# A linear-attention layer and a soft mixture of experts on one core: load ring, weight order and output queues changed

## The chip, the core and the metric

The kernel runs on one core of a Trainium2 chip. The metric is the device time of one execution in microseconds; a profile of one execution shows its span, that is the time from its first to its last instruction. The core has five engines that run side by side and wait for one another by semaphores: TensorE (PE, matrix products; PEld are its weight loads), VectorE (DVE), ScalarE (ACT), GpSimd (POOL) and SyncE (SP). SyncE, ScalarE and GpSimd can issue DMA transfers, which move data between HBM and the on-chip memory SBUF on 16 shared DMA engines. Matrix products land in PSUM.

## The reference

Two layers in a row. The first is a linear attention with decay, for 4 batches, 8 heads, 768 steps and head size 48 (float32):

```python
for t in range(S):
    kt, vt, rt = (k[:, :, t], v[:, :, t], r[:, :, t])
    cur = np.einsum('bhd,bhe->bhde', u[None] * kt, vt)
    y[:, :, t] = np.einsum('bhd,bhde->bhe', rt, state + cur)
    state = w[None, :, :, None] * state + np.einsum('bhd,bhe->bhde', kt, vt)
```

Its output, as 3072 rows x of 384, goes through a soft mixture of 8 experts with 4 slots each (phi is 384 x 32, w1 8 x 384 x 1024, w2 8 x 1024 x 384):

```python
logits = x @ phi
d = softmax of logits over the 3072 rows      # dispatch
slot_input = d.T @ x                          # 32 slots of 384
h = np.maximum(slot_input[e] @ w1[e], 0.0)    # for each expert e
slot_out[e] = h @ w2[e]
c = softmax of logits over the 32 slots       # combine
out = c @ slot_out
```

The two softmax lines are shortened here. All of x must be known before the experts can start, and the experts must be done before the first row of the output.

## The kernel before

**Stage 1, the chunks.** The 3072 rows are worked in 12 chunks of 256 rows (`nS`; three to a batch), two neighbouring rows to a partition (`J` = 2). The main loop (`for n in range(nS - 1)`, L538, and a tail for the last chunk) is software-pipelined: in iteration n it computes chunk n, prepares the transposes of n+1 and the products of n+3, and routes the rows of n-1. The order on each engine is that of the program. For each chunk:

- `mults` (L241) scales r, k by powers of the decay (L254, L256) and k by u (L257), on GpSimd, for chunk 0 on VectorE. `v_cast` (L264, ScalarE) makes v bf16. `r_copy`, `kur` and `dsum` (L277, L283, L294) form the term of the row with itself, and `dmul` (L301) its product with v. After `dsum` and `v_cast` nothing reads the loaded chunk any more.
- `trans` and `evac` transpose the scaled r and k (TensorE, ScalarE); `att` and `masks` (L331, L343) make the masked products within the chunk; `y_open`, `inter`, `state`, `intra` and `st_next` build the output and the state.
- `xt`, `lg`, `expo` make the logits of the rows and their exponentials; `disp` (L488, L491) adds the chunk's share to the slot inputs. There the rows x are the stationary operand of the matmul, loaded into TensorE 128 contiguous columns at a time.

**Loads.** r, k and v come by SyncE, in runs of 384 bytes. The pool `ld` has two buffers of a whole batch each. Batch 0 is loaded in nine transfers, one per chunk and tensor (`load_part`, L75), batches 1 to 3 in three each (`load`, L83). A later batch reuses the buffer of the batch two before it, so it waits for the last chunk of that one. The order is k, r, v.

**Weights.** w1 and w2 are read as float32 and cast to bf16 by transfers that GpSimd issues between its products (`load_w`), 0.79 MB of bf16 each: 8 blocks of w1, 7 of w2 and the last of w2 in four parts. How many go out at which iteration stands in the lists `W_IN` (inside `mults`) and `W_AT` (at the iteration's end); at iteration 8 all the rest. w2 of experts 4 to 7 (`w2_tail`) goes into a batch buffer of `ld`. For w1, input column `mo*128 + p` lies on partition p, so that each partition gets three runs of 4 KB; w2 has one run of 12 KB.

**Stage 2, the experts** (from `up`, L645): the up projections of four experts at a time (`up`, L652), transposes (`turn`), the down projections (`down`, L681), and the last expert's apart (`last_down`, L712), in the order in which its four parts land. `fill` and `keep` are padding matmuls on TensorE whose results nobody reads.

**Stage 3, the output:** 12 pieces of 256 rows. TensorE multiplies the combine weights by the slot outputs, VectorE scales the even rows of a piece (L745) and ScalarE the odd ones (L747), and SyncE sends it out, the first piece in two transfers (L749), the others in one of 384 KB (L751). The pool `ob` has six buffers.

Of the kernel before, what the change touches and what calls it, by code (L numbers as in the profile page):

```python
# [11 lines left out]
def kernel(  # L12
# [12 lines left out]
    nc = tc.nc  # L25
    B, H, S, D = r.shape
# [16 lines left out]
    P = 128  # L43
# [14 lines left out]
    w2_h = [wts.tile([P, E // 2, nF, Dm], bf, name="w2_h")[:]]  # L58
    ident = wts.tile([P, P], bf, name="ident")
    ld = ctx.enter_context(tc.tile_pool(name="ld", bufs=2))  # L60
    cst = ctx.enter_context(tc.tile_pool(name="cst", bufs=1))

    loads = {}

    SRC = ((1, k), (0, r), (2, v))

    def new_batch(b):
        bt = ld.tile([P, 3, H, nSb, J * D], f32, name="rkv")
        for i in range(nSb):
            loads[b * nSb + i] = [bt[:, x, :, i, :].rearrange("p h (j d) -> p j h d", j=J) for x in range(3)]  # L70
        return bt

    def load_part(bt, i):
        for x, src in SRC:
            nc.sync.dma_start(out=bt[:, x, :, i, :],  # L75
                              in_=src[0, :, i * TS:(i + 1) * TS, :].rearrange("h (p j) d -> p h (j d)", j=J))

    def load(b):
        if b >= B:
            return  # L80
        bt = new_batch(b)
        for x, src in SRC:
            nc.sync.dma_start(out=bt[:, x].rearrange("p h i m -> p (h i) m"),  # L83
                              in_=src[b].rearrange("h (i p j) d -> p (h i) (j d)", p=P, j=J))

    b_first = new_batch(0)
    load_part(b_first, 0)
# [14 lines left out]
    for i in range(1, nSb):  # L102
        load_part(b_first, i)
    load(1)
# [71 lines left out]
    w1_ap = moe_w1.rearrange("e (mo p) f -> p e mo f", p=P)  # L176
# [12 lines left out]
    def w2_load(e, f0=0, f1=nF):  # L189
        if e == XE and f0 == 0:  # L190
            tail = ld.tile([P, (E - XE) * nF * Dm], bf, name="w2_tail", tag="rkv",
                           padded_shape=[P, 3 * H * nSb * 2 * J * D])
            w2_h.append(tail[:].rearrange("p (e f d) -> p e f d", e=E - XE, f=nF))
        nc.gpsimd.dma_start(out=w2_h[e // XE][:, e % XE, f0:f1, :], in_=w2_ap[:, e, f0:f1, :])
# [5 lines left out]
    for f in range(0, nF, 2):  # L200
        w_todo.append((w2_load, (E - 1, f, f + 2)))
# [8 lines left out]
    with tc.tile_pool(name="wk", bufs=2) as wk, \  # L210
# [270 lines left out]
        def disp(n):  # L481
# [3 lines left out]
            for g in range(2):  # L485
                q = 2 * (n % 2) + g
                for mi in range(nM):
# [39 lines left out]
        dsum(0)  # L527
        mults(1)
        mults(2)
        load_w(2)  # L530
        trans(0, "kk")
        evac(0, "kk")
        trans(0, "rr")
# [248 lines left out]
```

## Time and profile before

| | us |
|---|---|
| median of 13 runs (lowest to highest) | 128.74 (127.67 to 137.31) |
| the profiled execution | 128.7 |
| its span | 126.5 |
| busy: PE / DVE / ACT / POOL | 98.0 / 92.3 / 78.9 / 77.7 |
| r, k, v, w1, w2 read (with the output, HBM read 39.38 MB, written 4.72 MB) | mean 349 GB/s over the span |

The profile gives for each engine its busy time and for each group of instructions its line, engine, operation and shapes. The slices cut the span into 40 equal parts; a digit is a share in tenths. Windows give the same for chosen stretches. An idle time stands in brackets after an instruction, with what ended it. The DMA rate counts what arrives, so a weight that is cast from float32 to bf16 counts with half of the bytes that were read. The DMA share can pass 1[...].

### The profile page before, as it was taken

Reading aid. Unit: us, or ns where it says so; the run is one execution under the profiler, and the core shown is the slowest. Engines: PE = TensorE matmul, PEld = TensorE weight load, DVE = VectorE, ACT = ScalarE, POOL = GpSimd, SP = SyncE. Lnnn points to the kernel's source line nnn. Section 1 sums busy time; section 2 is a strip of 40 time slices with the busy share of each in tenths; the row PEclk is TensorE's granted clock in tenths of the full one; section 3 lists DMA queues with packets and bytes.
Section 4 is the critical chain, followed back from the end, with each engine's and each line's share of the span. In section 5 each row is a group of like instructions: output and inputs, shape, how many; then the busy total and the mean of one; then the engine's idle time right before and its main releaser. Section 6 shows DMA issues by size and latency. Waiting matters only on the chain.

```text
span 126.5 us, 4177 instructions
## 1 busy us (share of the span) xinstructions
PE 98.0 (77%) x1779; PEld 70.5 (56%) x1779; DVE 92.3 (73%) x180; ACT 78.9 (62%) x143; POOL 77.7 (61%) x70
## 2 busy tenths in 40 slices
PE   3994899969597969079798959997999999794000
PEld 3493577756576757067676748775666566521000
DVE  5499988899999999385999997999662411375500
ACT  5869495869697967378688878788222320375500
POOL 6009999799998899997999999993410000000000
PEclk9999999999999999955999996799869999996555
DMA  3999999999999999999999999999999999049993
GB/s 83 301 325 324 334 327 271 310 212 230 286 301 282 235 256 265 343 296 267 243 253 254 239 211 225 216 213 219 214 211 212 218 204 167 4 150 394 400 401 154
DMA packets 23543, 31.78 MB, mean 251 GB/s; under 512 B 10450, under 2 KB 18132, under 8 KB 23524
## 3 DMA queue, kind: packets, MB, share of 16 engines
q0 software_dynamic: 4816, 12.63, 51.4%
q1 hardware_dynamic: 18288, 18.88, 47.0%
q8 instruction: 14, 0.23, 0.7%
q10 hardware_dynamic: 420, 0.00, 0.2%
q14 instruction: 5, 0.04, 0.1%
HBM read 39.38 MB, written 4.72 MB: 349 GB/s over the span
## 4 chain that ended last, share of the span: by engine, by line
PE 35%; DMA 23%; DVE 20%; SPq 8%; ACT 5%; issue 3%; ACTq 1%; DVEq 0%
DMA rkv<-in_v_dram 14%; SPq L83 8%; DMA out_dram<-o_s 6%; DVE at_s L343 6%; PE t_p L312 5%; DVE rpun L294 5%; PE aat_p L331 4%; DMA w_pd<-in_w_dram 3%; DVE dv L301 3%; PE xl_p L431 3%; DVE rkv L283 3%; PE y_p L352 2%; PE pad L517 2%; PE so_p L681 2%; PE rpun L488 2%
## 5 line engine op out<-in xcount | busy, mean ns | idle before, releaser
L343 DVE TENSOR_TENSOR at_s<-aat_p,mask 128x512 bf16<-128x512 f32 x47 | 30.2, 684 | 3.8 <-PE aat_p L331 3.6
L254 POOL TENSOR_TENSOR rr<-rkv,W_n 128x768 bf16<-128x768 f32 x11 | 20.0, 1822 | 9.1 <-DMA rkv<-in_r_dram 9.0
L257 POOL TENSOR_TENSOR rkv<-rkv,u_rep 128x768 f32<-128x768 f32 x11 | 19.9, 1809 | 0.9
L256 POOL TENSOR_TENSOR kk<-rkv,W_k 128x768 bf16<-128x768 f32 x11 | 20.0, 1818 | 0.1
L331 PE MATMUL aat_p<-t_rr,t_kk 64*64 64x128 bf16 x376 | 12.5, 249 | 9.0 <-ACT t_kk L319 6.3
L277 ACT COPY rpun<-rkv 128x384 f32<-128x384 f32 x23 | 11.3, 492 | 9.4 <-PE rpun L491 7.8
L331 PEld LDWEIGHTS <-t_kk 64*64 64x64 bf16 x384 | 8.7, 123 | 12.3 <-ACT t_kk L319 8.5
L301 DVE TENSOR_TENSOR dv<-v_bf,rpun 128x768 bf16<-128x768 bf16 x12 | 11.4, 954 | 3.1 <-ACT v_bf L264 2.1
L319 ACT COPY t_kk<-t_p 128x1024 bf16<-128x1024 bf16 x12 | 12.2, 1013 | 1.1 <-PE t_p L312 1.1
L283 DVE TENSOR_TENSOR rkv<-rkv,rpun 128x384 f32<-128x384 f32 x23 | 12.6, 546 | 0.2
L294 DVE TENSOR_REDUCE rpun<-rkv 128x16 f32<-128x768 f32 x12 | 11.5, 961 | 0.4
L264 ACT CAST v_bf<-rkv 128x768 bf16<-128x768 f32 x12 | 10.0, 830 | 2.9 <-DMA rkv<-in_v_dram 2.9
L319 ACT COPY t_rr<-t_p 128x1024 bf16<-128x1024 bf16 x11 | 11.2, 1017 | 0.5 <-PE t_p L312 0.3
L382 PE MATMUL s_p<-v_bf,kk 64*128 64x96 bf16 x160 | 11.4, 218 | 0.0
L391 DVE TENSOR_TENSOR st<-s_p,wm 128x384 bf16<-128x384 f32 x20 | 10.9, 546 | 0.5 <-PE s_p L382 0.3
L433 ACT COPY xt_s<-xl_p 128x768 bf16<-128x768 bf16 x11 | 8.8, 798 | 3.1 <-PE xl_p L431 3.0
L382 PEld LDWEIGHTS <-kk 64*128 64x128 bf16 x160 | 8.3, 102 | 3.8 <-issue 3.8
L745 DVE TENSOR_SCALAR o_s<-o_p,rsum_r 128x384 f32<-128x384 f32 x12 | 7.0, 615 | 4.3 <-DMA out_dram<-o_s 3.7
L412 ACT CAST x_t<-y_p 128x384 bf16<-128x384 f32 x22 | 9.6, 494 | 0.0
L747 ACT ACTIVATE o_s<-o_p,rsum_r 128x384 f32<-128x384 f32 x12 | 6.4, 584 | 4.7 <-DMA out_dram<-o_s 4.0
L488 PE MATMUL rpun<-Lexp,x_t 128*128 128x32 bf16 x66 | 5.2, 180 | 5.1 <-DVE dv L301 5.1
L312 PE MATMUL t_p<-ident,kk 128*128 128x128 bf16 x96 | 8.9, 248 | 0.2 <-ACT t_rr L319 0.2
(130 smaller groups left out, 188.0 us busy)
## 6 DMA issues: line engine op xcount, KB each, us to landing
w_all<-in_moe_w_dram POOLq DMA_DIRECT2D x8, 768.0 KB, 11.8
out_dram<-o_s SPq DMA_DIRECT2D x11, 384.0 KB, 4.3
w_h<-in_moe_w_dram POOLq DMA_DIRECT2D x4, 768.0 KB, 13.2
w_tail<-in_moe_w_dram POOLq DMA_DIRECT2D x3, 768.0 KB, 19.5
rkv<-in_k_dram SPq DMA_DIRECT2D x3, 384.0 KB, 4.4
rkv<-in_r_dram SPq DMA_DIRECT2D x3, 384.0 KB, 4.7
rkv<-in_v_dram SPq DMA_DIRECT2D x3, 384.0 KB, 5.0
w_tail<-in_moe_w_dram POOLq DMA_DIRECT2D x4, 192.0 KB, 21.0
```

The lines of the kernel that those rows point to most:

```text
L254: nc.gpsimd.tensor_mul(rr[:, :, :, 0:D], r_l, W_n[:])
L256: nc.gpsimd.tensor_mul(kk[:, :, :, 0:D], k_l, W_k[:])
L257: nc.gpsimd.tensor_mul(ku, ku, u_b)
L277: nc.scalar.copy(rp, loads[n][0][:, j, :, :])
L283: nc.vector.tensor_mul(s["ku"][:, j, :, :], s["ku"][:, j, :, :], s["rps"][j])
L294: nc.vector.tensor_reduce(d, s["ku"], axis=mybir.AxisListType.X, op=ALU.add)
L301: nc.vector.tensor_mul(dv[:], s["v"][:], d[:, :, :, None].to_broadcast([P, J, H, D]))
L312: nc.tensor.transpose(t_p[:, q, :, j, :], s[nm][:, j, 2 * q:2 * q + 2, :].rearrange("p h d -> p (h d)"), ident[:])
L319: nc.scalar.copy(t_s[:], s.pop("p_" + nm)[:])
L331: nc.tensor.matmul(at_p[a][g * HF:(g + 1) * HF, q, :], kT[sl, q, g, j, :], rT[sl, q, g, :, :].rearrange("p j c -> p (j c)"), start=True, s ...
L343: nc.vector.tensor_mul(s["at"][:, a, j, :, :], at_p[a][:], mask[:, j, None, :].to_broadcast([P, nP, P]))
L382: nc.tensor.matmul(s_p[:, q * D2:(q + 1) * D2], s["kk"][sl, j, 2 * q:2 * q + 2, :].rearrange("p h d -> p (h d)"), s["v"][sl, j, 2 * q:2 * ...
```

## The change

Five things change together.

- The pool `ld` becomes a ring of six buffers of one chunk each. A chunk is loaded by three transfers (for the first chunk k, r, v, for the others r, k, v). Six chunks are asked for at the start, chunk 6 after `v_cast(0)`, and chunk n+7 at the end of iteration n. w2 of experts 4 to 7 takes four buffers of the ring.
- Weights are issued at other iterations: one block instead of two before the loop, and new lists `W_IN` and `W_AT`. The last block of w2 comes in three parts (4, 2 and 2 of 8 columns of F/128), and `last_down` takes the first four in one go.
- Column `p*3 + mo` of the input now lies on partition p for w1, so each partition gets one run of 12 KB. To match it, the dispatch matmuls take every third column of x as stationary operand.
- Output pieces 2, 4, 6, 8 and 10 are sent by GpSimd, the others by SyncE, and `ob` has 12 buffers.
- Each half of the first output piece is scaled in two column halves, one on VectorE and one on ScalarE.

```diff
-    w2_h = [wts.tile([P, E // 2, nF, Dm], bf, name="w2_h")[:]]
+    w2_h = wts.tile([P, E // 2, nF, Dm], bf, name="w2_h")
+    w2_of = [w2_h[:, e] for e in range(E // 2)]
-    ld = ctx.enter_context(tc.tile_pool(name="ld", bufs=2))
+    ld = ctx.enter_context(tc.tile_pool(name="ld", bufs=6))
...
-    def load(b):
-        if b >= B:
-            return
-        bt = new_batch(b)
-        for x, src in SRC:
-            nc.sync.dma_start(out=bt[:, x].rearrange("p h i m -> p (h i) m"),
-                              in_=src[b].rearrange("h (i p j) d -> p (h i) (j d)", p=P, j=J))
-
-    b_first = new_batch(0)
-    load_part(b_first, 0)
+    def load(n):
+        if n >= nS:
+            return
+        b, i = divmod(n, nSb)
+        bt = ld.tile([P, 3, H, J * D], f32, name="rkv")
+        loads[n] = [bt[:, x].rearrange("p h (j d) -> p j h d", j=J) for x in range(3)]
+        for x, src in SRC if n == 0 else (SRC[1], SRC[0], SRC[2]):
+            nc.sync.dma_start(out=bt[:, x],
+                              in_=src[b, :, i * TS:(i + 1) * TS, :].rearrange("h (p j) d -> p h (j d)", j=J))
+
+    load(0)
...
-    for i in range(1, nSb):
-        load_part(b_first, i)
-    load(1)
+    for n in range(1, NL):
+        load(n)
...
-    w1_ap = moe_w1.rearrange("e (mo p) f -> p e mo f", p=P)
+    w1_ap = moe_w1.rearrange("e (p mo) f -> p e mo f", p=P)
...
     def w2_load(e, f0=0, f1=nF):
-        if e == XE and f0 == 0:
-            tail = ld.tile([P, (E - XE) * nF * Dm], bf, name="w2_tail", tag="rkv",
-                           padded_shape=[P, 3 * H * nSb * 2 * J * D])
-            w2_h.append(tail[:].rearrange("p (e f d) -> p e f d", e=E - XE, f=nF))
-        nc.gpsimd.dma_start(out=w2_h[e // XE][:, e % XE, f0:f1, :], in_=w2_ap[:, e, f0:f1, :])
+        if e >= XE and f0 == 0:
+            tail = ld.tile([P, nF * Dm], bf, name="w2_tail", tag="rkv", padded_shape=[P, 2 * 3 * H * J * D])
+            w2_of.append(tail[:].rearrange("p (f d) -> p f d", f=nF))
+        nc.gpsimd.dma_start(out=w2_of[e][:, f0:f1, :], in_=w2_ap[:, e, f0:f1, :])
...
-    for f in range(0, nF, 2):
-        w_todo.append((w2_load, (E - 1, f, f + 2)))
+    for f0, f1 in ((0, 4), (4, 6), (6, nF)):
+        w_todo.append((w2_load, (E - 1, f0, f1)))
...
+                x_v = x_of[n][g].rearrange("p (c m) -> p m c", m=nM)
                 for mi in range(nM):
-                    nc.tensor.matmul(un_p[:, mi * ES:(mi + 1) * ES], x_of[n][g][:, mi * P:(mi + 1) * P], le[:, q, :],
+                    nc.tensor.matmul(un_p[:, mi * ES:(mi + 1) * ES], x_v[:, mi, :], le[:, q, :],
...
-        W_IN = [0, 0, 1, 0, 0, 1, 1, 1, 1]
-        W_AT = [0, 0, 1, 0, 0, 1, 1, 1, 3, 0, 0]
+        W_IN = [0, 0, 1, 0, 1, 1, 1, 1, 1]
+        W_AT = [0, 0, 0, 0, 1, 1, 1, 1, 2, 0, 0]
...
-        load_w(2)
+        load_w(1)
...
         v_cast(0)
+        load(NL)
...
-            if n % nSb == 1:
-                load(n // nSb + 2)
+            load(n + 1 + NL)
...
-        last_down(0, 2)
         keep(2)
-        last_down(2, 4)
+        last_down(0, 4)
         keep(1)
...
-    with tc.tile_pool(name="ob", bufs=6) as ob, \
+    with tc.tile_pool(name="ob", bufs=12) as ob, \
...
+            put = nc.gpsimd.dma_start if i and i % 2 == 0 else nc.sync.dma_start
             for j in range(J):
...
+                parts = ((0, HD), (HD, Dm)) if i == 0 else ((0, Dm),)
+                for c, (d0, d1) in enumerate(parts):
+                    o_p = out_ps.tile([P, Dm], f32, name=f"o_p{2 * j + c if i == 0 else 2 * qh + j}")
+                    for q2 in range(2):
...
+                    if (c if i == 0 else j) == 0:
+                        nc.vector.tensor_scalar_mul(o_s[:, j, d0:d1], o_p[:, d0:d1], sc_col)
+                    else:
+                        nc.scalar.activation(out=o_s[:, j, d0:d1], in_=o_p[:, d0:d1], func=AF.Copy, scale=sc_col)
                 if i == 0:
-                    nc.sync.dma_start(out=out_ap[i][:, j, :], in_=o_s[:, j, :])
+                    put(out=out_ap[i][:, j, :], in_=o_s[:, j, :])
             if i > 0:
-                nc.sync.dma_start(out=out_ap[i], in_=o_s[:])
+                put(out=out_ap[i], in_=o_s[:])
```

## The prediction

> **What bounds the kernel now.** The profiled execution took 128.7 us, equal to the median of the 13 runs (128.74), and its span is 126.5 us; 2.2 us lie around the span. I read the page's slices first.
>
> ```profile
> DMA  3999999999999999999999999999999999049993
> GB/s 83 301 325 324 334 327 271 310 212 230 286 301 282 235 256 265 343 296 267 243 253 254 239 211 225 216 213 219 214 211 212 218 204 167 4 150 394 400 401 154
> ```
>
> A slice is 3.16 us. No compute engine is full, but the DMA row is full from slice 1 to slice 33, drops to nothing once, and is full again in the output. So I asked for windows: the end of the weight stream, and the start of the output (columns: busy time of five engines, granted clock, DMA share, GB/s).
>
> ```profile
> 105.00:106.00 1.00, 1.00 (x22) 0.65 (x24) 0.00 (x0) 0.00 (x0) 0.00 (x0) 1.00 1.16 207
> 106.00:107.00 1.00, 1.00 (x15) 0.58 (x10) 0.52 (x1) 0.00 (x0) 0.00 (x0) 1.00 0.86 152
> 107.00:108.00 1.00, 1.00 (x13) 0.91 (x11) 0.04 (x1) 0.00 (x0) 0.00 (x0) 1.00 0.32 57
> ...
> 112.00:113.00 1.00, 0.97 (x10) 0.26 (x8) 1.00 (x3) 0.96 (x3) 0.00 (x0) 1.00 0.46 163
> 113.00:114.00 1.00, 0.66 (x6) 0.13 (x4) 0.11 (x1) 0.00 (x0) 0.00 (x0) 1.00 0.38 141
> 114.00:115.00 1.00, 0.00 (x0) 0.00 (x0) 0.27 (x1) 0.29 (x1) 0.00 (x0) 0.82 1.03 399
> ```
>
> The transfers stop at 107.3. The last piece of the last w2 block, asked for alone in the view of one tile, was issued at 90.0 and landed 18.4 us later:
>
> ```profile
> L194 POOL DMA_DIRECT2D w_tail<-in_moe_w_dram x1: 528/528/528, 90.0 to 90.0; - x1
> DMA to landing us min/median/max: 18.4/18.4/18.4
> ```
>
> That is 108.4, and the last four `sr_p` matmuls, which read it, stand on TensorE at 108.50 to 108.93. The chain of waits names TensorE from 89 to 109, but part of that is padding (`pad_f`); the piece cannot be used sooner. So DMA and compute reach 108.5 together.
>
> The accounts of the stream: r, k, v are 14.16 MB and ran at 325 to 336 GB/s when alone (windows from 6 to 18 us): 43.2 us at 328. The weights arrive as 12.58 MB of bf16 at 214 GB/s when alone (211 to 221 from 78 to 96 us): 58.8 us. From a start at 2.4 us, with the 1.0 us between last transfer and landing, 105.4 us would be the landing without loss; it was 108.4. Some 3.0 us are lost. The DMA share is low, 0.94 to 1.03 against 1.08 to 1.19 elsewhere, in 18–24, 33–39 and 54–57 us: there SyncE passes from one batch load to the next.
>
> In the middle the compute really stalls. VectorE (time, duration, line, and in brackets its idle time and releaser):
>
> ```profile
> 48.32 1.29 DVE L343 TENSOR_TENSOR at_s<-aat_p,mask 128x512 bf16<-128x512 f32 x2
> ...
> 53.58 0.95 DVE L301 TENSOR_TENSOR dv<-v_bf,rpun 128x768 bf16<-128x768 bf16 x1 [2.06 <-ACT v_bf L264]
> ...
> 58.32 1.29 DVE L343 TENSOR_TENSOR at_s<-aat_p,mask 128x512 bf16<-128x512 f32 x2 [1.37 <-PE aat_p L331]
> ```
>
> Two equal points of successive chunks lie 10.0 us apart; elsewhere this period is 6.4 to 6.5. The stall is 3.5 us: v of batch 2, issued at 35.6 behind k and r of the same batch, landed at 52.7.
>
> **What the Trainium skill says.** "DMA: Bandwidth & Descriptors", section "Issuing engines are not separate DMA queues": another issuing engine saves only sequencer time, since all share the same engines. The trace agrees where the queue is full (output at 393 to 406 GB/s from 114 us); but at 112 to 114 sequencer time is what is missing. "SBUF — State Buffer", section "Door 1: The DMA port swizzle": accesses want at least two hits per 16-byte line. The trace agrees for one stride (below). "TensorE: Matmul & The Clock Gate", section "Part 1: The HAM clock gate": an idle window of about 3.4 us halves the clock. The trace shows more sensitivity: after 3.6 us idle at 51–54.5 the clock was 0.5 from 53.4 to 60, after some 1.5 us of idle time around 74.5 it was 0.5 from 77.4 to 80.7.
>
> **The change, part by part.**
>
> *Ring of six chunk buffers.* It removes the batch waits: SyncE waited 11.8 us for `rpun` L294 before L83, 6.5 us longest. Chunk 6 was issued from 26.0, after chunk 2 was finished; now it may follow chunk 5 at about 20, since chunk 0 is done at 12.1. One chunk costs 14.16/12/0.328 = 3.6 us of DMA, one weight block 58.8/16 = 3.7 us, one period 6.5. Counting chunks 0–5 from 2.4 us, one weight block and chunk 6, the DMA has work to about 31 us; chunks 7, 8, 9 are freed at about 18, 26 and 32, ahead of need. Compute loses its 3.5 us stall. That is worth nothing directly, because the weights land no sooner for it. Its cover is the weight stream; were that shorter, up to 3.5 us would come out. What changes the end is the 3.0 us lost by the DMA: many 384 KB loads in turn instead of three batch bursts. Bounds 0 and −3.0, and a loss is excluded only if no buffer wait starves the queue, which the count above says. I take a third, −1.0 us: the boundaries vanish, while mixing of the two queues stays.
>
> *The moved weight issues* (fewer early, more from chunk 4 on) put r, k, v ahead. GpSimd has 8 issues of 0.80 us for w1; with 12 KB runs instead of 4 KB the nearest row is w2's 0.60: 8 × 0.2 = 1.6 us less GpSimd time. With r loaded first, `rr` of chunk 1 can start when the slot issued at 3.0 lands (8.4 instead of 9.7). GpSimd finished `rkv` L257 of the last chunk at 80.1 and this is needed around 84: worth 0, cover is VectorE's period. w1 alone arrived at the same 207 to 221 GB/s (73–77 us) as w2, so longer runs gain 0 in bandwidth; bounds 0 to −0.5.
>
> *w2 tail in four ring buffers:* their chunks 6 to 9 are over before GpSimd gets there (after about 75 us), 0. The last block in pieces of 4, 2, 2: the last piece has the same size, 0. One issue of 0.55 us goes.
>
> *Strided stationary reads* (every third bf16, 6 bytes, in the dispatch matmuls). Trace: `h_s` loads at 16-byte stride took 151 ns (L667), contiguous `x_t` of the same shape 105 (L431). So 0 to +46 ns for each of 72 loads, at most 0.28 us per chunk and 3.3 in all. I take little, since 6 bytes leave over two hits per line; it comes off the 3.5 us of compute slack, not off the end.
>
> *Output.* Twelve buffers remove 7.7 us of waits by VectorE and ScalarE for output DMAs, 0 for the end: DMA is full then. First piece in halves: 0.42 us (the `so_r` row, 192 columns) instead of 0.62 and 0.58, so about −0.2 to the first issue at 110.52. Then this SyncE line:
>
> ```profile
> L751 SPq DMA_DIRECT2D out_dram<-o_s x1: 1706/1706/1706, 111.5 to 111.5; - x1
> ```
>
> One issue of 1.71 us (median 0.88) let the DMA run at 163 and 141 GB/s for 2 us: at 400 this is 2 − 304/400 = 1.2 us lost. In the new kernel GpSimd issues piece 2, ready near 111.7, behind nothing (its last copies ended at 92.3), at about 0.55 us an issue; data flow about 1 us sooner. Bounds: −1.4 (all of it and the halves) and +0.3 (slower first byte from GpSimd). I take −0.8 − 0.2 = −1.0.
>
> Sum: span 126.5 − 1.0 − 1.0 = 124.5; with 2.2 around it 126.7 us.
>
> **Rivals.** (1) *A short cold clock at the tail.* Compute arrives 3.5 us early, so TensorE idles 2 to 3 us before the second down projection; its last weight block lands near 103.3. From there to the end it has 4.04 us of full-speed work, 1.41+0.33+0.88+0.16+0.17+0.33+0.33+0.43. If half clock sets in at 104.5 for 3.4 us, the end comes at about 109.0, as before: only the output's gain is left, 127.7. For it: the events at 77 and 91 us; against: padding matmuls. (2) *Everything recovered:* DMA −3.0, output −1.4: 124.3. Against: mixing. (3) *Nothing moves:* the losses are mixing, and GpSimd's first byte is no sooner: 128.5. (4) *Slower: a long cold clock.* At 51–54 a 3.6 us pause gave 6.6 us of half clock. If the pause before the second down projection passes about 3 us, the 4.04 us take 8.1: end at 103.3 + 8.1 = 111.4 against 108.9, +2.5, less 1.0 of output: 130.2. Against: the pause must be that long, that is no compute given back to strided loads.
>
> **How the numbers follow.** A measurement here can tell about 0.5% (128.1 to 129.4 is no change). Main forecast 126.7 with 0.50 (own range 125.6 to 127.6), rival 1 0.22, rival 2 0.12, rival 3 0.08, rival 4 0.08. Below 125.0 lies most of rival 2, above 128.8 rival 4 and a little of rival 3; so 125.0 to 128.8. Faster: 0.50 + 0.12 + 0.15 of rival 1 = 0.77; same: 0.07 of rival 1 and most of rival 3, 0.14; slower 0.09.
>
> **What would show it.** Right: no long gap of VectorE near 51–58; second `at_s` period even at 6.5; r, k, v all landed before about 60; the last w2 piece landing near 107.4; TensorE waiting for w2 before the last down matmuls; DMA above 350 GB/s from the second microsecond of the output. Wrong: a DMA share below 1.0 in the middle, new waits of SyncE for DMA landings, half clock between 103 and 109, output slices under 390 GB/s, or weights landing far earlier than 107, which would say that the stream wasn't the bound.

## The result: 9% slower

The changed kernel takes 140.92 us (median of 11 runs, 139.12 to 149.29), the kernel before, on the same chip, 129.10. The ratio is 1.0916, with a 95% interval of 1.0872 to 1.0960. Predicted were 126.7 us and a range of 125.0 to 128.8. The profiled execution took 140.67 us with a span of 138.9 (before: 126.5), so 12.4 us of span are to be found. Repeated runs of a kernel scatter upward, so the ratios and intervals here compare only the runs within 1.5% of a kernel's fastest, and where only one of four runs lies there the runs are listed without an interval.

### Where the time stands

The two slice rows of the page of the kernel after; a slice is 3.47 us:

```profile
DMA  3999999989999999999999999949899999019993
GB/s 101 301 325 325 325 276 198 234 228 251 251 253 264 254 191 240 221 214 231 290 237 252 217 214 220 230 92 200 148 189 212 212 210 166 17 63 383 386 394 140
```

The DMA is still full nearly everywhere. But beside the short gap before the output there is now a hole in slices 26 to 29 (92, 200, 148, 189 GB/s, at 90 to 104 us), and before it the rate is no better than it was. The last parts of the last w2 block, from the view of one tile, late in the loop:

```profile
L184 POOL DMA_DIRECT2D w_tail<-in_moe_w_dram x2: 578/583/588, 101.2 to 101.7; - x2
...
DMA to landing us min/median/max: 18.5/18.7/18.9
```

They were issued at 101.2 and 101.7, where the last issue of the kernel before stands at 90.0, and the last landed at some 120.4 instead of 108.4. That is the 12 us. The weights did not take longer on their way (18.5 to 18.9 us against 18.4): they were asked for later. The main loop shows the same delay. Its last result, `unsiT`, is copied at 97.13 before and at 110.40 after, 13.3 us later:

```profile
97.13 0.36 DVE L614 CAST unsiT<-rpun 128x192 bf16<-128x192 f32 x1 [1.13 <-PE rpun L491]
```

```profile
110.40 0.36 DVE L605 CAST unsiT<-rpun 128x192 bf16<-128x192 f32 x1 [1.14 <-PE rpun L482]
```

From there to the first output issue it takes 13.10 us instead of 13.39, and from that issue to the end 15.4 instead of 16.0. 13.27 − 0.29 − 0.6 = 12.4: everything is lost in the main loop, and what follows it gave a little back.

### Who is late first

GpSimd issues the weights. Its view of the timeline after, cut to its weight issues and its two long waits (start, duration, line; in brackets the idle time before it and who ended it):

```profile
49.26 0.59 POOL L178 DMA_DIRECT2D w_all<-in_moe_w_dram  x1
...
51.63 0.57 POOL L178 DMA_DIRECT2D w_all<-in_moe_w_dram  x1
...
55.89 0.59 POOL L178 DMA_DIRECT2D w_all<-in_moe_w_dram  x1
66.27 1.80 POOL L244 TENSOR_TENSOR rr<-rkv,W_n 128x768 bf16<-128x768 f32 x1 [9.79 <-DMA rkv<-in_r_dram]
...
89.87 1.80 POOL L244 TENSOR_TENSOR rr<-rkv,W_n 128x768 bf16<-128x768 f32 x1 [10.40 <-DMA rkv<-in_r_dram]
91.63 0.57 POOL L184 DMA_DIRECT2D w_h<-in_moe_w_dram  x1
```

Twice GpSimd stands for about 10 us because r has not landed. Behind the waiting `rr` stand the next weight issues; at 90 us all the earlier blocks have arrived (the last at 89.1), and so the DMA runs dry until GpSimd has issued again. In the view of waits, all that GpSimd waited for r, before and then after (total, number of waits, longest):

```profile
POOL rr L254 <- DMA rkv<-in_r_dram: 9.0, 4, 6.9
```

```profile
POOL rr L244 <- DMA rkv<-in_r_dram: 25.9, 3, 10.4
```

Five to seven of these are the start of the kernel. VectorE after, which waits in turn:

```profile
72.37 0.55 DVE L273 TENSOR_TENSOR rkv<-rkv,rpun 128x384 f32<-128x384 f32 x1 [3.90 <-POOL rkv L247]
...
89.48 0.95 DVE L291 TENSOR_TENSOR dv<-v_bf,rpun 128x768 bf16<-128x768 bf16 x1 [5.90 <-ACT v_bf L254]
...
95.96 0.56 DVE L273 TENSOR_TENSOR rkv<-rkv,rpun 128x384 f32<-128x384 f32 x1 [3.58 <-POOL rkv L247]
```

The old stall near 51 to 58 is smaller, as predicted in part: two equal points of successive chunks lie 7.5 us apart there (48.52 and 56.03), 10.0 before and about 6.4 elsewhere. With

```profile
62.47 1.29 DVE L333 TENSOR_TENSOR at_s<-aat_p,mask 128x512 bf16<-128x512 f32 x2
```

VectorE is even 2.3 us ahead of the kernel before, where the same point stands at 64.75. From there to `unsiT` it loses 15.6 us: 13.4 in the three waits above, 0.7 in one more for `rkv`, and 1.5 in longer waits for TensorE, whose granted clock was 0.50 from 76 to 90 and from 99 to 104 us. A slower TensorE clock, as a rival cause, is thus worth 1.5 us at most directly.

Why does r land late? It was asked for 11 us before GpSimd stood ready for it (at 56.5 and 79.5 us). SyncE after:

```profile
21.59 4.92 SPq L76 DMA_DIRECT2D rkv<-in_v_dram  x1
26.64 3.38 SPq L76 DMA_DIRECT2D rkv<-in_r_dram  x1
...
45.10 1.70 SPq L76 DMA_DIRECT2D rkv<-in_r_dram  x1
...
50.06 13.02 SPq L76 DMA_DIRECT2D rkv<-in_v_dram  x1
...
68.67 1.21 SPq L76 DMA_DIRECT2D rkv<-in_r_dram  x1
69.92 15.55 SPq L76 DMA_DIRECT2D rkv<-in_k_dram  x1
```

The r asked for at 45.10 landed at 66.2, the one asked for at 68.67 at 89.8: 21.1 us each from issue to landing. The same loads of 384 KB took 4.9 to 5.1 us when asked for from 8 to 14 us, without weights beside them, and then one landed every 1.2 us. In between, single issues on SyncE took 13.02 and 15.55 us. Meanwhile the weights went through almost unhindered: blocks landed at 54.0, 58.1, 62.2 and 66.1, one in 4.0 us, and later at 85.4 and 89.1. Each r lands within 0.7 us after a weight block, at the moment when no further block is open. So r, k, v hardly get a share beside the weights; they are all but shut out. In the window 54.0 to 66.1 the DMA brought 222 GB/s; the three weight blocks are 195 of it (0.786 MB each), which leaves 27 for r, k, v. In the kernel before, r, k, v had much more: from 35.7 to 51.8, at 270 GB/s in all, two blocks landed (98 GB/s), and 172 were left.

The page's part on the queues shows what is different (packets, MB, share of the 16 engines); q1 is SyncE's, q0 GpSimd's. Before:

```profile
q0 software_dynamic: 4816, 12.63, 51.4%
q1 hardware_dynamic: 18288, 18.88, 47.0%
```

After:

```profile
q0 software_dynamic: 3024, 14.60, 49.4%
q1 hardware_dynamic: 38592, 16.91, 44.0%
```

The same r, k, v go in twice as many packets. A chunk load travels in packets of one 384-byte run; a batch load, whose runs are the same 384 bytes, had its packets filled with four of them (1536 bytes: 10.62 MB of batch loads in about 6900 packets, an estimate that takes 9216 packets for batch 0 and some 2160 for the output and the ends of the transfers off the 18288). And w1 goes in fewer, larger packets: a run of 12 KB, cast, is written as one packet of 6144 bytes, a run of 4 KB as one of 2048.

### The profile page after: what moved, and what is told of

It is laid out like the page before. It is cut to its first block, busy times and chain, and to the rows that moved or that the text cites. A ratio compares the mean times of both kernels' runs of the same rounds, so it can differ in the third digit from the quotient of the medians.

```text
span 138.9 us, 4185 instructions
## 1 busy us (share of the span) xinstructions
PE 101.7 (73%) x1783; PEld 73.3 (53%) x1783; DVE 93.3 (67%) x181; ACT 78.5 (57%) x144; POOL 78.8 (57%) x74
## 4 chain that ended last, share of the span: by engine, by line
DVE 25%; PE 23%; DMA 18%; SPq 16%; issue 4%; ACT 3%; POOL 3%; ACTq 1%; DVEq 0%; POOLq 0%
SPq L76 16%; DMA rkv<-in_v_dram 15%; DVE at_s L333 5%; DVE rpun L284 4%; DVE dv L291 4%; DVE o_s L738 4%; DVE rkv L273 3%; DMA w_pd<-in_w_dram 3%; PE pad L508 2%; PE so_p L672 2%; PE h_p L643 2%; DVE rkv L242 2%; DVE st L381 2%; PE t_p L302 2%; PE rpun L479 2%
## 5 line engine op out<-in xcount | busy, mean ns | idle before, releaser
L246 POOL TENSOR_TENSOR kk<-rkv,W_k 128x768 bf16<-128x768 f32 x11 | 20.8, 1887 | 0.1
L744 POOL DMA_DIRECT2D out_dram<-o_s x5 | 2.7, 545 | 23.3 <-DVE o_s L738 22.8
L372 PE MATMUL s_p<-v_bf,kk 64*128 64x96 bf16 x160 | 12.0, 225 | 0.0
L394 PE MATMUL y_p<-v_bf,at_s 64*128 64x48 bf16 x384 | 8.6, 192 | 3.9 <-DVE at_s L333 3.8
L372 PEld LDWEIGHTS <-kk 64*128 64x128 bf16 x160 | 8.8, 106 | 4.2 <-issue 4.1
L394 PEld LDWEIGHTS <-at_s 64*128 64x128 bf16 x384 | 6.8, 100 | 6.4 <-DVE at_s L333 4.4
```

The lines of the kernel that those rows point to most:

```text
L246: nc.gpsimd.tensor_mul(kk[:, :, :, 0:D], k_l, W_k[:])
L372: nc.tensor.matmul(s_p[:, q * D2:(q + 1) * D2], s["kk"][sl, j, 2 * q:2 * q + 2, :].rearrange("p h d -> p (h d)"), s["v"][sl, j, 2 * q:2 * ...
L394: nc.tensor.matmul(s["y"][g][:, h * D:(h + 1) * D], s["at"][sl, a, j, q, :], s["v"][sl, j, h, :], start=False, stop=(a == 1 and q == nP - ...
```

## The experiments

Two theories. **T:** while both queues have work, they take turns packet by packet, so that bytes are shared in the ratio of the packet sizes. That was 1536 to 2048 before (0.75) and is 384 to 6144 after (0.06). **L:** only some eight transfers are served at a time, and blocks that are open crowd the others out whatever their pieces. The expectations of e1 to e3 use other letters: R blames the long runs of w1 and P the small packets of the chunk loads, the two halves of T; O blames the ring and the moved issues and not the packets. In m1's, S has the two queues share evenly when they are alone.

### The parts, one at a time

**e1_after_4k_runs:** the changed kernel with w1 in three runs of 4 KB, kept apart by 16 unused columns.

```diff
-    w1_all = wts.tile([P, E, nM, F], bf, name="w1_all")
+    w1_all = wts.tile([P, E, nM, F + 16], bf, name="w1_all")
...
-        nc.gpsimd.dma_start(out=w1_all[:, e, :, :], in_=w1_ap[:, e, :, :])
+        nc.gpsimd.dma_start(out=w1_all[:, e, :, 0:F], in_=w1_ap[:, e, :, :])
```

> The changed kernel, with w1's rows in SBUF 16 elements apart from one another, so that each partition's transfer is three runs of 4 KB again and nothing else differs (layout, strided reads, order, ring and queues stay). Theory R (w1's 12 KB runs take the turns of the DMA engines from r, k, v): the two GpSimd waits for r, 20.2 us together, fall under 5 us and the time to 126 to 131 us. Theory P (the loads of one chunk make packets of 384 bytes, those of a batch larger ones, and the small packets lose whatever the weights' runs are): waits above 10 us, time 135 us or more. Theory O (the ring and the moved weight issues are to blame, the packets not): 139 to 141 us.

Measured: 158.74, 133.44, 135.96, 142.62 us. No interval can be formed, and no range of R, P or O holds all four. The lowest run is 5.6 us above the lowest of the kernel before beside it (127.83) and 5.7 below that of the changed kernel (139.12). So smaller w1 pieces seem to help but don't cure it; w2, which makes up the later part of the weights, still has 12 KB runs here.

**e2_before_12k_runs:** the kernel before with w1 in one run of 12 KB, and the strided dispatch that belongs to it.

```diff
-    w1_ap = moe_w1.rearrange("e (mo p) f -> p e mo f", p=P)
+    w1_ap = moe_w1.rearrange("e (p mo) f -> p e mo f", p=P)
...
+                x_v = x_of[n][g].rearrange("p (c m) -> p m c", m=nM)
...
-                    nc.tensor.matmul(un_p[:, mi * ES:(mi + 1) * ES], x_of[n][g][:, mi * P:(mi + 1) * P], le[:, q, :],
+                    nc.tensor.matmul(un_p[:, mi * ES:(mi + 1) * ES], x_v[:, mi, :], le[:, q, :],
```

> The kernel before with the w1 part of the change alone: 12 KB runs and the strided stationary reads in the dispatch. Theory R: r of batches 2 and 3 lands only when the weights in flight have landed, 134 us or more. Theory P: batch loads still hold their own, 128 to 131 us. Theory O: 128 to 130 us. In all of them the strided reads cost under 1 us.

Measured: 131.15, 137.46, 135.69, 128.46 us beside 129.2; no interval. In the profile of the first run GpSimd's waits for r are 13.9 us, against 9.0 before. But the lowest run is within 0.6 us of the lowest before (127.83), so a cost of this part alone isn't shown.

**e3_before_chunk_loads:** the kernel before, where each batch is loaded by nine chunk transfers instead of three. Buffers, bytes and 384-byte runs stay the same.

```diff
-        for x, src in SRC:
-            nc.sync.dma_start(out=bt[:, x].rearrange("p h i m -> p (h i) m"),
-                              in_=src[b].rearrange("h (i p j) d -> p (h i) (j d)", p=P, j=J))
+        for i in range(nSb):
+            load_part(bt, i, b)
```

> The kernel before, with batches 1 to 3 loaded by nine transfers each, one per chunk and tensor, into the same two batch buffers; w1 stays at 4 KB runs. Theory R: 127 to 130 us. Theory P: hardware-queue packets rise from 18288 to about 38600, r, k, v lose their turns, 134 us or more. Theory O: 127 to 130 us.

Measured: 144.06 us, ratio 1.1139 (1.1053 to 1.1226). This one edit costs more than the whole change. SyncE's queue and GpSimd's waits in e3:

```profile
q1 hardware_dynamic: 39312, 18.88, 46.9%
```

```profile
POOL rr L253 <- DMA rkv<-in_r_dram: 26.9, 4, 14.1
```

The packets double, the waits triple, and the loads asked for from 62.7 to 78.2 us landed at 91 to 93.3, when the last full weight block (90.1) was through: the picture of the changed kernel, without ring, lists or 12 KB runs in w1.

**e4_before_output:** the kernel before with the output part alone (12 buffers, pieces in turn from SyncE and GpSimd, the first in column halves).

```diff
-    with tc.tile_pool(name="ob", bufs=6) as ob, \
+    with tc.tile_pool(name="ob", bufs=12) as ob, \
...
+            put = nc.gpsimd.dma_start if i and i % 2 == 0 else nc.sync.dma_start
...
-                nc.sync.dma_start(out=out_ap[i], in_=o_s[:])
+                put(out=out_ap[i], in_=o_s[:])
```

> The kernel before with the output part of the change alone (first piece in column halves on two engines, twelve buffers, pieces in turn from SyncE and GpSimd). By the prediction's sum for this part 1.0 us less than before, 128.1 us, with data above 350 GB/s from the second microsecond of the output; by the rival that GpSimd's queue is of no use 129.1 us; in the changed kernel the output ran at 380 to 386 GB/s where the one before had 395 to 400, so a loss of up to 0.5 us is possible too.

Measured: 128.02 us, ratio 0.9891 (0.9860 to 0.9921): 1.4 us gained (1.0 to 1.8). It is small but clear of the scatter, and the version to keep.

### Sizes or numbers

**e5_after_short_runs:** the changed kernel with short weight runs: w1 written in pieces of 512 bytes, w2 of 768.

```diff
-    w1_all = wts.tile([P, E, nM, F], bf, name="w1_all")
-    w2_h = wts.tile([P, E // 2, nF, Dm], bf, name="w2_h")
+    w1_all = wts.tile([P, E, nM, 4, F // 4 + 4], bf, name="w1_all")
+    w2_h = wts.tile([P, E // 2, nF, Dm + 4], bf, name="w2_h")
```

> The changed kernel with weights in short runs: w1 comes in pieces of 256 columns (1 KB read, 0.5 KB written), w2 in rows of 384 (1.5 KB read, 0.75 KB written), by small gaps between the rows in SBUF; the order, the ring and the 384-byte packets of r, k, v stay. Theory T (DMA engines take turns by packets, so the queue with the smaller packets loses in proportion): the packets are now nearly equal, r, k, v get about half, the GpSimd waits for r after 50 us fall from 20.2 us to under 4, and the time goes to 125 to 131 us, or some more if 16 blocks with 4 to 8 times the packets cost GpSimd over 1 us each. Rival L (SyncE lets only eight transfers be open, and eight chunk loads are a third of eight batch loads, so r, k, v are asked for too late): the waits stay over 15 us and the time over 138.

Measured: 144.39 us, ratio 1.1153 (1.1017 to 1.1288); `unsiT` at 104.15, 6 us sooner than in the changed kernel. r, k, v now kept 85 to 90 GB/s beside weights at 110 to 114, and GpSimd's waits for r fell to 11.1 us, 5 of them after the start: the shutting out is gone, as T says. The time is a miss for T all the same (125 to 131 was expected). Such small pieces carry less in all (200 GB/s from 57.6 to 86.3 us), the last w2 landed at about 123, 2.6 us later than in the changed kernel, and the stream of bytes set the end. The share was cured and the time was not.

**e6_after_weights_last:** no weights before iteration 8.

```diff
-        W_IN = [0, 0, 1, 0, 1, 1, 1, 1, 1]
-        W_AT = [0, 0, 0, 0, 1, 1, 1, 1, 2, 0, 0]
+        W_IN = [0, 0, 0, 0, 0, 0, 0, 0, 0]
+        W_AT = [0, 0, 0, 0, 0, 0, 0, 0, 0, 0, 0]
...
-        load_w(1)
```

> The changed kernel with all weight blocks asked for at iteration 8, none before. It will be slow, since 58.8 us of weights start at about 70 us: 145 to 155 us. What tells is the main loop: by theory T the 384-byte loads alone keep up, GpSimd waits for r only at the start, and the last dispatch (where the unsiT copy of VectorE stands at 97.1 us in the kernel before and near 110.6 in the changed one) comes at 91 to 94 us. By rival L the waits for r stay (over 8 us after the start), and it comes after 100.

Measured: 158.01 us, ratio 1.2170 (145 to 155 was expected); the DMA stands still from 53 to 75 us. What counts is the loads. From the view of waits, and two windows (busy of five engines, clock, DMA share, GB/s):

```profile
POOL rr L244 <- DMA rkv<-in_r_dram: 5.9, 1, 5.9
```

```profile
20.00:35.00 15.00, 12.62 (x271) 9.69 (x270) 13.77 (x22) 11.03 (x20) 14.84 (x9) 0.85 1.07 285
...
52.60:98.90 46.30, 41.71 (x830) 32.15 (x828) 37.80 (x64) 31.91 (x59) 26.21 (x25) 0.82 0.51 104
```

With the same chunk loads and ring, but no weights beside them, every load was in by 52.6 us and GpSimd waited for none after the start. Chunk loads by themselves did no harm. The loop was not done at 91 to 94 as expected, though, but at 98.9 (`unsiT`), with a granted clock of 0.82. So without any wait for loads after the start the loop took no less than before (97.1): the "3.5 us of compute slack" of the prediction did not come out here.

**e7_before_half_heads:** the batch loads of the kernel before, cut by heads into two of 576 KB.

```diff
-            nc.sync.dma_start(out=bt[:, x].rearrange("p h i m -> p (h i) m"),
-                              in_=src[b].rearrange("h (i p j) d -> p (h i) (j d)", p=P, j=J))
+            for h0 in range(0, H, H // 2):
+                nc.sync.dma_start(out=bt[:, x, h0:h0 + H // 2].rearrange("p h i m -> p (h i) m"),
+                                  in_=src[b, h0:h0 + H // 2].rearrange("h (i p j) d -> p (h i) (j d)", p=P, j=J))
```

> The kernel before, with each batch load of a tensor split in two, by heads: 576 KB each, 12 runs of 384 bytes on a partition instead of 24. It asks what makes the larger packets. By theory T the time follows the packet count of SyncE's queue: near 18300 packets, 128 to 131 us; near 38600, 139 to 146 us. By rival L the time lies between, 131 to 137 us, whatever the packets are.

Measured: 135.24 us, ratio 1.0491 (1.0420 to 1.0563), with 39168 packets on SyncE's queue. A transfer with 12 runs to a partition goes in 384-byte packets like one with 8; only one with 24 had four runs to a packet. The time is a miss for T, which wanted 139 to 146 us with that many packets, and lies in the range of L (131 to 137). The packets alone thus don't set the loss: with the same ones e3 costs 8.8 us more. Stage D below, where half batches keep the same share as chunk loads, speaks for T's sharing; why half batches cost less in the kernel stays open.

### The packet ratio, measured alone

**m1_two_queues** and **m2_two_queues** contain transfers only. In m1 the stages slid by one another, which paired other sizes than meant; m2 ties each stage, so that both queues start together.

> The two queues alone, without any of the layer's computation (it leaves out everything but transfers; the output is written as zeros). Six stages one after the other; in each GpSimd asks for six weight blocks at once (4.7 MB of bf16) and SyncE for 4.7 MB of r, k, v: A chunk loads beside 12 KB weight runs, B chunk loads beside 4 KB runs, C chunk loads beside 1 KB runs, D batch loads beside 12 KB runs, E batch loads beside 4 KB runs, F half-batch loads beside 4 KB runs. Theory T (turns by packets, the smaller packets lose): in A the r, k, v loads get under 40 GB/s while weights are in flight and land after them, in B under 60, in C about 90; in D and E, where the packets are 1.5 KB, above 90; F like B. Rival L (eight open transfers): A, B and C alike, D and E better, F between. Rival S (it needs the compute engines' waits, the queues alone share evenly): about half the time each in all six stages.

> Transfers only: all products, gates, scales and outputs are left out, so its time says nothing of the kernel. In each stage both queues start together: chunk or batch loads of r, k, v on the SyncE queue beside weight blocks on the GpSimd queue, with one pairing of piece sizes per stage. If the two queues take turns packet by packet (T), bytes go as the packet sizes do. A, chunk loads beside w1 in 4 KB runs: weights about 177 GB/s, r, k, v about 38. B, batch loads beside 12 KB runs (ratio 1536/6144): 180 and 45. C, batch loads beside runs that write 1 KB (ratio 1.5): 95 and 140. D, half-batch loads beside 4 KB runs: as A, since both have 384-byte packets. E, chunk loads beside 12 KB runs: 200 and 10. F, chunk loads alone: 262. G, batch loads alone: 276. H, w1 in 4 KB runs alone: 214. If the number of open transfers decided instead (L), A, B, D and E would share about alike, near half and half.

Windows of m2, in the order A, B, C, D, E, F, G, taken where both queues (in F and G the one) had work (busy of VectorE and GpSimd, clock, DMA share, GB/s):

```profile
5.00:29.00 24.00, 0.77 (x5) 0.98 (x2) 1.00 1.13 211
48.00:69.00 21.00, 0.77 (x5) 0.00 (x0) 1.00 1.04 235
91.00:110.00 19.00, 0.31 (x2) 0.00 (x0) 1.00 1.15 269
131.00:155.00 24.00, 0.80 (x6) 0.00 (x0) 1.00 1.12 214
172.00:192.00 20.00, 0.77 (x5) 0.00 (x0) 1.00 1.04 217
212.00:226.00 14.00, 0.46 (x3) 0.00 (x0) 1.00 1.28 263
236.00:249.00 13.00, 0.46 (x3) 0.00 (x0) 1.00 1.10 261
```

A small VectorE instruction reads one element of each weight block when it has landed, so the intervals of the blocks can be read off; for stage E the first and the last of six:

```profile
172.69 0.15 DVE L98 CAST see<-wE 128x1 f32<-128x1 bf16 x1 [7.33 <-DMA wE<-in_moe_w_dram]
...
192.32 0.15 DVE L98 CAST see<-wE 128x1 f32<-128x1 bf16 x1 [3.82 <-DMA wE<-in_moe_w_dram]
```

Five blocks in 19.63 us: 3.93 us a block, 200 GB/s; of the 217 in the window 17 are left for r, k, v. In the same way:

| stage: loads beside w1 runs | packets, bytes | ratio | us a block | weights, GB/s | r, k, v, GB/s | measured ratio |
|---|---|---|---|---|---|---|
| A: chunk, 4 KB | 384 / 2048 | 0.19 | 4.46 | 177 | 35 | 0.20 |
| B: batch, 12 KB | 1536 / 6144 | 0.25 | 4.28 | 184 | 51 | 0.28 |
| C: batch, 2 KB | 1536 / 1024 | 1.50 | 7.29 | 108 | 161 | 1.49 |
| D: half batch, 4 KB | 384 / 2048 | 0.19 | 4.47 | 176 | 38 | 0.22 |
| E: chunk, 12 KB | 384 / 6144 | 0.06 | 3.93 | 200 | 17 | 0.08 |
| H: none, 4 KB | – | – | 3.71 | 212 | – | – |

T fits closely in all five. L, which wanted near halves in A, B, D and E, falls as an account of the shares, and so does S. m1 had the pairing of the kernel before, batch loads beside 4 KB runs:

```profile
158.00:184.00 26.00, 0.31 (x2) 0.00 (x0) 1.00 1.10 252
```

Six blocks landed from 158.5 to 185.9, 5.5 us apart (143 GB/s), which leaves 109 for r, k, v, a ratio of 0.76 (packets: 0.75). The Trainium skill has this mechanism in "DMA: Bandwidth & Descriptors", section "Queues, rings and completion order": each DMA engine goes round the queue rows that have work "at *packet* granularity". The shares above agree with that if a packet is what the profile counts as one, a single 384-byte run or four; the page's typical packet, of about 9 to 17 descriptors, is not what the counts here show. The prediction named another section of that page and passed this one over. Note also the cost to the other side: beside chunk loads with 12 KB runs the weights still run at 200 of their 212 GB/s. They hardly notice the loads.

### The weight lists

**e8_after_old_lists:** the changed kernel with the old lists (two blocks ahead of the loop).

```diff
-        W_IN = [0, 0, 1, 0, 1, 1, 1, 1, 1]
-        W_AT = [0, 0, 0, 0, 1, 1, 1, 1, 2, 0, 0]
+        W_IN = [0, 0, 1, 0, 0, 1, 1, 1, 1]
+        W_AT = [0, 0, 1, 0, 0, 1, 1, 1, 3, 0, 0]
...
-        load_w(1)
+        load_w(2)
```

> The changed kernel with the weight issues at the iterations of the kernel before (two blocks ahead of the loop, the old W_IN and W_AT). By theory T the moved issues are not the cause: the stalls stay, 138 to 146 us. If the moved issues were what let the weights in front of r, k, v, it would fall to 128 to 132 us.

Measured: 134.08 us, ratio 1.0282 (1.0153 to 1.0411). Of the 11.8 us lost 3.7 are left (2.0 to 5.3, from two runs), so undoing the moved weight issues alone gives back about 8. It lies between the two expectations (128 to 132 and 138 to 146): the moved issues are a cause, which T's expectation denied.

**e9_before_new_lists:** the reverse, the new lists alone in the kernel before.

```diff
-        W_IN = [0, 0, 1, 0, 0, 1, 1, 1, 1]
-        W_AT = [0, 0, 1, 0, 0, 1, 1, 1, 3, 0, 0]
+        W_IN = [0, 0, 1, 0, 1, 1, 1, 1, 1]
+        W_AT = [0, 0, 0, 0, 1, 1, 1, 1, 2, 0, 0]
...
-        load_w(2)
+        load_w(1)
```

> The kernel before with the new weight lists alone (two r, k, v loads and one block ahead of the loop, the other blocks at later iterations); batch loads and 4 KB runs stay, with packets of 1536 and 2048 bytes. T: the ratio .75 leaves r, k, v about 109 GB/s beside the weights, GpSimd waits for r no more than 10 us in all, and the time is 128 to 132 us. If several open blocks are enough to shut r, k, v out whatever the packets, 135 us or more, with waits for r above 18 us.

Measured: 135.57, 139.19, 134.71, 132.21 us beside 129.54; no interval, but the lowest is 4.0 us above the lowest before (128.22). The time lies between the two expectations or above, and GpSimd's waits for r, 17.1 us in the profile of the first run, are a miss for T (10 at most). The share came out as T wants it: the blocks landed at 60.7, 66.2, 71.7 and 77.2, 5.5 us apart (143 GB/s), and the window from 55.1 to 79.5 has 246 in all, so 103 for r, k, v, where m1 gave 109. What T's arithmetic left out is the rest: a batch needs 3.54 MB, at 103 to 109 GB/s some 33 us. r of batch 3, asked for at 49.5, landed at 68.3, v at 79.5. In the kernel before, with two blocks issued at 35.6 and 40.1 and none until 54.2, r, k, v had 172 GB/s. Here four blocks are issued between 49 and 61 us, before batch 3 is in, and then even the old packets are too slow for the loop.

**e10_after_batch_loads:** all of the change except the ring: batch loads, two buffers.

```diff
-    ld = ctx.enter_context(tc.tile_pool(name="ld", bufs=6))
+    ld = ctx.enter_context(tc.tile_pool(name="ld", bufs=2))
...
-            load(n + 1 + NL)
+            if n % nSb == 1:
+                load(n // nSb + 2)
```

> All of the change but the ring: two batch buffers and batch loads as before, with the new weight lists, 12 KB runs for w1, strided reads, r first, w2 in three parts and the output on two queues. Theory T: without the small packets nothing is shut out, and the gain of the output stays: 127 to 129.5 us. If the new weight lists or the 12 KB runs are enough to shut out r, k, v: 133 us or more.

Measured: 133.85, 137.36, 137.22, 138.5 us beside 129.2; expected was under 129.5, a miss. e9 and stage B give a likely reason: the lists cost by themselves, and beside 12 KB runs a batch load keeps only 51 GB/s. r of batch 3, asked for at 45.8, landed at 65.4.

**e11_after_weights_later** and **e12_after_weights_later2:** the changed kernel with blocks moved from iterations 4 to 5 and beyond.

```diff
-        W_IN = [0, 0, 1, 0, 1, 1, 1, 1, 1]
-        W_AT = [0, 0, 0, 0, 1, 1, 1, 1, 2, 0, 0]
+        W_IN = [0, 0, 1, 0, 0, 1, 1, 1, 1]
+        W_AT = [0, 0, 0, 0, 0, 2, 2, 2, 2, 0, 0]
```

(e12: `[0, 0, 1, 0, 0, 2, 1, 1, 1]` and `[0, 0, 0, 0, 0, 2, 2, 2, 1, 0, 0]`.)

> The changed kernel with the weight issues moved so that few are open while chunk loads are on the way: one before the loop and one at iteration 2 as in it, then none until the chunk loads have been asked for, 1 and 2 at iteration 5, three at each of 6, 7 and 8. Theory T: with an empty weight queue the loads get through (all landed near 53 us, as with the weights last), the two long waits of GpSimd for r are gone, and the DMA then has 14 blocks of 3.7 us from about 52 us: the last lands near 106, the time 124.5 to 128 us. Rival L: a wait for r over 5 us stays, 131 us or more.

> As the one before, but with two weight blocks inside iteration 5 instead of one, and one less at iteration 8, so that the DMA is fed 3 us earlier. Theory T: 124 to 127.5 us where the last chunk loads are already through at about 52 us; if not, a wait for r or k of up to 5 us comes back and it is the slower of the two, 128 to 132.

Measured: 142.52, 142.75, 142.96, 135.57 us, and 148.15, 145.87, 146.21, 140.11 us, beside 129.21. Both missed, by their lowest runs too: I had taken the last chunk loads to be in by then. In the profile of e11 the ring asks for the last two chunks only from 49.3 and 55.7 us on, and the blocks opened from 50.7 on shut them out again; a v asked for at 52.6 landed at 91.9. GpSimd's waits for r were 19.5 and 19.4 us.

**e13_output_short_runs:** the output part, with w1 written in pieces of 1 KB, which turns the ratio to 1.5 (and the strided dispatch that belongs to this order of w1).

```diff
-        nc.gpsimd.dma_start(out=w1_all[:, e, :, :], in_=w1_ap[:, e, :, :])
+        nc.gpsimd.dma_start(out=w1_all[:, e, :, :, 0:F // 2].rearrange("p m c f -> p (m c) f"),
+                            in_=w1_ap[:, e, :, :].rearrange("p m (c f) -> p (m c) f", c=2))
```

> The kernel before with the output part of the change, and with w1 stored in 2 KB runs (1 KB written), so that the batch loads have the larger packets (ratio 1.5). T: the r of a batch that is loaded beside weights lands sooner and GpSimd's wait for it is shorter; the time is 126.5 to 128.5 us, beside 128.0 for the output part alone. If smaller weight pieces lose more in the mix than the loads gain, as with 1 KB and 1.5 KB runs before, it is 129 us or more, with the last w2 block later than 108.

Measured: 129.15 us, ratio 0.9935 (0.9907 to 0.9964). In its profile GpSimd's waits for r are 8.6 us and `unsiT` comes at 95.18, sooner than in the kernel before, and v of the last batch landed at 69.1 instead of 73.1, so the loads do gain a little. But the last w2 still landed at 108.4, and the gain is, if anything, smaller than e4's. A loop that ends 2 us sooner was worth nothing there, which is what the prediction said of the stall.

### What adds up

| | us beside the kernel before |
|---|---|
| output part alone (e4) | −1.4 |
| new lists alone (e9) | +4.0, lowest runs |
| 12 KB runs alone (e2) | +0.6, lowest runs |
| chunk loads alone (e3) | +14.7 |
| all without the ring (e10) | +5.2, lowest runs |
| all with w1 in 4 KB runs (e1) | +5.6, lowest runs |
| all with the old lists (e8) | +3.7 |
| all | +11.8 |

"Lowest runs" compares the lowest of four runs with the lowest of the kernel before beside it, has no interval, and says little below 1 us. The parts don't add: chunk loads alone cost more than all together, and undoing any one of three parts (e1, e8, e10) gives back about half or more; a likely reason is that all three delay the same loads. e8 has the same 384-byte packets as e3 and larger weight pieces, yet costs 11 us less, of which the output part explains 1.4. Why is not settled: the ring, the order with r first and the runs of w1 differ together, and the ring does not ask for its loads sooner (chunks 6 and 8 from 29.5 and 45.7 us in e8, from 25.2 and 42.0 in e3).

## Why the prediction was wrong

- *DMA stream as the bound, last w2 at 108.4.* Right for the kernel before, as far as e13 tells: a loop that ends 2 us sooner moved nothing while the last w2 landed at the same 108.4.
- *Ring: −1.0 from the DMA, "a loss is excluded only if no buffer wait starves the queue, which the count above says".* **This step failed.** The count of buffers was right: those of chunks 0 to 3 were free after `dsum` at 13.4, 19.5, 26.0 and 32.4 us (counted: 12.1, 18, 26 and 32). But SyncE's issues stood back to back, and single ones took 3.3 to 4.9 us from the moment the first weight block was open (issued at 20.26), so it came to chunks 6 to 9 only at 26.6, 32.6, 38.7 and 45.1. Chunk 6 was thus asked for no sooner than before (26.0). Above all the step took a transfer that is asked for as one that is served. Chunk loads double the number of packets; with a full weight queue beside them r, k, v get 17 to 35 GB/s instead of 109 (E, A, m1). The queue that starved was no queue without buffers, it was one without turns. And what starved in the end was the other one: GpSimd, which waits for r, issues the weights. In place of −1.0 us, chunk loads alone cost 14.7 (e3), and with them the whole change came to +11.8.
- *Moved weight issues "put r, k, v ahead": 0.* **Failed as well:** undone, some 8 us come back (e8). They open four blocks between 45 and 56 us, when chunks 9 to 11 and v of chunk 8 still have to come. The cover named for GpSimd, VectorE's period, holds for its busy time; what stands behind a GpSimd that waits, the weight issues, wasn't counted.
- *12 KB runs: 0 in bandwidth.* Right for weights alone, and the wrong question: the piece size sets the share (0.20 in A against 0.08 in E). What it is worth in the kernel is not settled (e1, e2).
- *Strided stationary reads: little.* Right: the dispatch loads took 97 ns before and 107 after, and those of `xl_p`, which weren't changed, 105 and 112; by the medians 96 and 104 against 98 and 98, so the stride costs some 8 ns a load, an estimated 0.6 us for all 72.
- *Output: −1.0.* Right in sign, and near in size: −1.4 (−1.0 to −1.8) in e4. GpSimd issues a piece in 0.55 us. The first issue is at 123.50; where the DMA brought 163 and 141 GB/s from 1.5 to 3.5 us after it, it now brings about twice as much, by the windows after:

```profile
124.00:126.00 2.00, 1.96 (x22) 0.56 (x17) 2.00 (x5) 2.00 (x6) 0.56 (x1) 1.00 0.86 306
126.00:127.00 1.00, 0.97 (x10) 0.21 (x9) 1.00 (x3) 1.00 (x4) 0.55 (x1) 1.00 0.99 367
```

- *Compute has 3.5 us to spare.* Not shown. Without waits for loads after the start the loop ended at 98.9 (e6, with a clock of 0.82), with shorter waits at 95.2 (e13), against 97.1.
- *Rivals.* None was the case. All four took the stream's total as given and differed only at its tail; the rival on the slower side, a long cold clock, was looked for in the wrong place. Of the signs named for "wrong", the DMA share below 1.0 came (0.61 to 0.76 from 90 to 99 us), and so did output slices under 390 GB/s (383 and 386) and a half clock, though mostly earlier (76 to 90). SyncE was held up in issues of 13.02 and 15.55 us, and not in waits for landings.

What stays open: why half batches (e7) cost less than chunk loads (e3) with the same packets; why a batch load gets packets of four runs and a half batch doesn't (24 and 12 runs to a partition); and why r, k, v ran at 325 to 336 GB/s at the start of the kernels, but at 261 to 263 alone in m2.

## What to carry over

Where two DMA queues are busy at once, compare the packet sizes of their pieces, as the profile's count of packets and bytes gives them: here the bytes were shared in that ratio, and at 0.06 the queue with the small packets was all but shut out as long as the other had blocks open. Keep transfers that feed the critical chain in large packets, or leave stretches without bulk loads, as the kernel before does between 40 and 54 us; e11 and e12 show that such a stretch has to lie where the small loads are really asked for. And when an engine both waits for data and issues transfers, add up what stands behind the wait.

## What was not expected of the hardware

- Loads with the same 384-byte runs went in packets of 384 bytes with 8 or 12 runs to a partition, and of 1536 with 24. For the sharing this is a factor of four.
- A queue with larger packets is hardly slowed: weights at 200 GB/s beside chunk loads and 212 alone, while chunk loads fell from 263 to 17.
- The profile's DMA share passes 1 with a single queue at work too: 1.28 for chunk loads alone (F).
- The total depends on the mix: 269 GB/s for batch loads beside 1 KB pieces (C), 211 to 217 for chunk loads beside larger ones (A, E), 200 in e5.
